# Overlapping the first attention block with the LayerNorm and V prologue, with V computed by head group

## The chip, the cores and the metric

The kernel runs on one core of one Trainium2 chip. The metric is the device time of one execution in microseconds (us), as a median of several executions. All executions used here agree within about 0.7% per kernel. ScalarE is written ACT in the profile, VectorE is DVE, GpSimd is POOL, TensorE is PE with its weight loads apart as PEld, and the DMA queue is SP.

## The reference

The sum of three terms is computed for x of 1x2048x512 in bfloat16:

```python
xn = layernorm(x)
q, k, v = split(xn @ wqkv)            # 32 heads of 16
A = concat_heads(softmax(q k^T / 4) v) @ wo
h = layernorm(xn)                      # "LN2" below
u = gelu(einsum("bsd,sf->bdf", h, w1) + b1)
B = (einsum("bdf,fs->bds", u, w2) + b2).transpose(0, 2, 1)
out = x + A + B
```

## The kernel before

A host-side scheduler writes one instruction list per engine, and every engine executes its list in order. A dependence between engines becomes a semaphore wait in front of the later instruction. So an instruction waits for all that was *emitted* before it on its own engine, whether it needs it or not.

The attention has 32 blocks of four heads. A block has 16 *periods*. In each period TensorE computes four score tiles (two pairs), ScalarE takes two exps of 128x1024, and TensorE multiplies the exps of two periods earlier with V ("PV"). Up to two further matmuls of 512 columns per period are taken from a queue of extra tasks: the K projection of later head groups (`kt`), Q projections (`qt`), the feed-forward parts (`ut`, `yt`) and the output projection (`op`). These share one PSUM bank (`EX_BANK`), so the next task's matmul waits until VectorE has evicted the one before.

The parts that matter (cut):

```python
def ln_stats(t, which):     # VectorE: statistics; POOL: (var + eps) ** -0.5
    dve.bn_stats(...); dve.bn_aggr(...)
    pool.tensor_scalar(... EPS ...); pool.tensor_tensor(... ALU.pow)
def ln_norm(t, which):      # VectorE, waits for POOL
    dve.tensor_scalar(dst[:, t, :], src[:, t, :], mean, rstd, ALU.subtract, ALU.mult)

# prologue, all 16 tiles before the first exp
for s_ in range(NT + 4):
    if s_ < NT: ln_stats(s_, 0)                        # statistics of the new tile first
    t = s_ - 1: ln_norm(t, 0); transpose_pe(t, t % 2)  # then the previous tile's normalize
    t = s_ - 2: transpose_copy(...); v_pe(t, ...); kt_pe(0, t // 4, ...) every fourth
    t = s_ - 3: v_evac(t, ...); kt_evac(...) every fourth
qt_proj(0, 0, EX_BANK)
late_consts()               # POOL: two memsets of wo_pad, then its loads

def task_ln2():             # one tile per period, from period 0 of block 0
    for t in range(NT):
        yield 0.0
        ln_stats(t, 1); ln_norm(t, 1)

# main loop, per period: scores, two exps, PV of period-2, then extra tasks
def exp_pair(n):
    act.activation(pT[:, buf, :], ps[...1024 columns...], ACTF.Exp, scale=0.25)
```

The softmax here doesn't subtract the row's maximum and nothing guards it: scores larger than these inputs give would overflow.

Of the kernel before, what the change touches and what calls it, by code (L numbers as in the profile page):

```python
# [13 lines left out]
D = 512  # L14
# [166 lines left out]
def bass_parallel_sum__softmax_full_mha__mixer_token_mlp__prompt_kernel(  # L181
# [18 lines left out]
    with ExitStack() as es:  # L200
# [48 lines left out]
        def bank(i):  # L249
            return ps[:, i * 512:(i + 1) * 512]  # L250
# [21 lines left out]
        sc.add("pool", lambda e: e.memset(mhalf[:], -0.5), writes=[("mhalf",)])  # L272
        sc.add("dve", lambda e: e.memset(b1c_bf[:], 0.0), writes=[("b1c",)])
        v17_main = V17[:, 0:NKT * H * 17].rearrange("p (n c) -> p n c", c=17)
        sc.add("dve", lambda e: e.memset(v17_main[:, :, 16:17], 1.0), writes=[("Vone",)])
        sc.add("dve", lambda e: e.memset(V17[:, NKT * H * 17:], 0.0), writes=[("Vpad",)])

        sc.add("pool", lambda e: e.memset(qmask[:, 0:1], 0.0), writes=[("qmask",)])
        for r in range(4):
# [72 lines left out]
        def transpose_pe(t, bk):  # L352
            for ct in range(NCT):
                sc.add("pe", lambda e, ct=ct: e.transpose(  # L354
                    ps_bf[:, bk * 1024 + ct * 128: bk * 1024 + (ct + 1) * 128],
                    xn_sb[:, t, ct * 128:(ct + 1) * 128], ident[:]),
                    reads=[("xn", t), ("ident",)], writes=[("bank", bk)])

        def transpose_copy(t, bk, eng):
            dst = xnT[:, :, t * 128:(t + 1) * 128]  # L360
            src = ps_bf[:, bk * 1024: bk * 1024 + 512].rearrange("p (ct j) -> p ct j", ct=NCT)
            evac(eng, dst, src, reads=[("bank", bk)], writes=[("xnT", t)])
# [10 lines left out]
        def kt_pe(T, c, bk):  # L373
            for _ in kt_pe_gen(T, c, bk):
                pass
# [10 lines left out]
        def evac(eng, dst, src, reads, writes):  # L386
            if eng == "act":
                return sc.add("act", lambda e: e.activation(dst, src, ACTF.Identity), reads=reads, writes=writes)  # L388
            return sc.add("dve", lambda e: e.tensor_copy(dst, src), reads=reads, writes=writes)  # L389
# [18 lines left out]
                                                                        None, ALU.mult),  # L408
                       reads=[("bank", bk), ("qmask",)], writes=[("QT", slot)])

        def v_tile(t, bk, evac_eng="dve"):
            v_pe(t, bk)
            v_evac(t, bk, evac_eng)

        def v_evac(t, bk, evac_eng):
            dst = V17[:, t * H * 17:(t + 1) * H * 17].rearrange("p (h c) -> p h c", c=17)[:, :, 0:16]
            src = bank(bk).rearrange("p (h d) -> p h d", d=16)
            evac(evac_eng, dst, src, reads=[("bank", bk)], writes=[("V", t)])

        def v_pe(t, bk):  # L420
            for ct in range(NCT):
                sc.add("pe", lambda e, ct=ct: e.matmul(  # L422
                    bank(bk), lhsT=xnT[:, ct, 128 * t:128 * (t + 1)], rhs=wqkv_sb[:, ct, 2 * D:3 * D],
                    start=(ct == 0), stop=(ct == NCT - 1)),
                    reads=[("wqkv", 2), ("xnT", t)], writes=[("bank", bk)])

        for s_ in range(NT + 4):
            if s_ < NT:
                ln_stats(s_, 0)
            t = s_ - 1  # L430
            if 0 <= t < NT:
                ln_norm(t, 0)
                transpose_pe(t, t % 2)
            t = s_ - 2
            if 0 <= t < NT:
                transpose_copy(t, t % 2, "act")
                v_pe(t, 2 + (t % 2))
                if t % 4 == 3:
                    kt_pe(0, t // 4, 4 + ((t // 4) % 2))
            t = s_ - 3  # L440
            if 0 <= t < NT:
                v_evac(t, 2 + (t % 2), "dve" if t % 4 == 1 else "act")
                if t % 4 == 3:
                    kt_evac(0, t // 4, 4 + ((t // 4) % 2), "act")
        qt_proj(0, 0, EX_BANK)
        late_consts()

        def task_ln2():
            for t in range(NT):
# [3 lines left out]
        def task_qt(arg):  # L453
            qb, T = arg
            yield from qt_proj_gen(qb, T, EX_BANK)

        def task_kt(T):
            for c in range(4):
# [154 lines left out]
            T, e_ = divmod(G, 2)  # L613
            return b, kt, qb, G, T, e_

        def score_group(g):
            b, kt, qb, G, T, e_ = blk_of(g)
            slot_q = b % NQS
            for r in range(4):
                n = 2 * g + r // 2  # L620
                s_ = n % 3
                bk = 2 * s_ + (r % 2)
                sc.add("pe", lambda e, r=r, bk=bk: e.matmul(  # L623
                    bank(bk), lhsT=KT[32 * r:32 * r + 32, T, 128 * kt:128 * (kt + 1)],
                    rhs=QT[32 * r:32 * r + 32, slot_q, :], start=True, stop=True,
                    tile_position=(32 * r, 0)),
                    reads=[("KT", T, kt // 4), ("QT", slot_q)], writes=[("bank", bk)], name="sc")

        def exp_pair(n):
            s_ = n % 3  # L630
            buf = n % NPB
            sc.add("act", lambda e: e.activation(pT[:, buf, :], ps[:, s_ * 1024:(s_ + 1) * 1024], ACTF.Exp, scale=0.25),  # L632
                   reads=[("bank", 2 * s_), ("bank", 2 * s_ + 1)], writes=[("pT", buf)], name="exp")

        def pv_group(g):
            b, kt, qb, G, T, e_ = blk_of(g)
            for r in range(4):
                n = 2 * g + r // 2
                buf = n % NPB
                h = 8 * T + 2 * r + e_  # L640
                off = (kt * H + h) * 17
                sc.add("pe", lambda e, r=r, buf=buf, off=off: e.matmul(  # L642
                    bank(PV_BANK)[32 * r:32 * r + 32, :], lhsT=V17[:, off:off + 32],
                    rhs=pT[:, buf, 512 * (r % 2):512 * (r % 2 + 1)],
                    start=(kt == 0), stop=(kt == NKT - 1), tile_position=(0, 32 * r)),
                    reads=[("V", kt), ("pT", buf), ("Vone",)] + ([("V", kt + 1)] if kt + 1 < NKT else [("Vpad",)]),
                    writes=[("bank", PV_BANK)], name="pv")

        def P(b, kt=0):
            return b * NKT + kt  # L650
# [5 lines left out]
                if b > 0:  # L656
                    sched_list.append((P(b - 1, 1), 0, "qt", (qb, T)))
        for T in range(1, 4):
            sched_list.append((P(2 * T - 2, 2), 1, "kt", T))
        for ft in range(NFT):  # L660
            sched_list.append((P(1, 4) + 6 * ft, 2, "ut", ft))
        for st in range(NT):
# [9 lines left out]
        def start_task(kind, arg):  # L672
            if kind == "qt":
                return task_qt(arg)
            if kind == "kt":
                return task_kt(arg)
            if kind == "ut":
                return task_ut(arg)
            if kind == "yt":
                return task_yt(arg)  # L680
            if kind == "op":
                return task_outproj(*arg)
            raise ValueError(kind)
# [9 lines left out]
                self.req = next(self.gen, None)  # L693

        bank_q = []
        free_tasks = [Task("ln2", None, task_ln2())]
        sl_idx = 0
        w1_loaded = 0
        w2_loaded = 0
        period = 0  # L700
        END = NGRP + LAG + 1
        while True:
            if period == P(0, 8):
                for ft in range(min(NW1, NFT)):
                    task_w1_load(ft)
                w1_loaded = min(NW1, NFT)
            if period == P(3, 0):
                for st in range(min(NW2, NT)):
                    task_w2_load(st)
                w2_loaded = min(NW2, NT)  # L710
            if period < NGRP:
                score_group(period)
                exp_pair(2 * period)
                exp_pair(2 * period + 1)
            for gp in (period - LAG - 1, period - LAG):
                if not (0 <= gp < NGRP):
                    continue
                b, kt = divmod(gp, NKT)
                due = gp + LAG + (1 if (kt == 0 and b > 0) else 0)
                if due != period:  # L720
                    continue
                pv_group(gp)
                if kt == NKT - 1:
                    if b == NBLK - 1:
                        assert sl_idx >= len(sched_list) and not any(tk.kind == "op" for tk in bank_q), \
                            "pre-accumulation of the last q block must be complete before the tail"
                        tail_epilogue(b)
                    else:
                        epilogue_copy(b)
                        free_tasks.append(Task("epi", b, task_epilogue_rest(b)))  # L730
            while sl_idx < len(sched_list) and sched_list[sl_idx][0] <= period:
                _, _, kind, arg = sched_list[sl_idx]
                tk_new = Task(kind, arg, start_task(kind, arg))
                if kind in ("qt", "kt"):
                    pos_ins = 1 if bank_q and bank_q[0].started else 0
                    while pos_ins < len(bank_q) and bank_q[pos_ins].kind in ("qt", "kt"):
                        pos_ins += 1
                    bank_q.insert(pos_ins, tk_new)
                else:
                    bank_q.append(tk_new)  # L740
                sl_idx += 1
# [93 lines left out]
```

## Time and profile before

| | before |
|---|---|
| median of 6 runs | 1007.68 us (1007.08 to 1010.33) |
| span of the profiled run | 1005.3 us |
| ScalarE busy | 968.6 us (96%) |
| first exp starts | 38.07 us |
| exp 32 (block 1) starts, counted from the timeline | 70.5 us |
| exp 72 starts, counted likewise | 108.9 us |

Exps are numbered from 0 to 1023. These lines of the profile page give busy time of the engines, the chain of work that ended last (by line), and the group of the exps.

```profile
PE 859.5 (85%) x4832; PEld 194.9 (19%) x4832; DVE 293.4 (29%) x472; ACT 968.6 (96%) x1068; POOL 71.0 (7%) x110
...
ACT pT L632 81%; PE ps L623 3%; PE ps L642 2%; PE ps L399 1%; DVE stats L329 1%; DVE big L344 1%; PE ps L484 1%; PE ps L422 1%; POOL mv L335 1%; PE ps L530 1%; ACT ga_sb L499 1%; PE ps L381 0%; DVE mv L331 0%; POOL mv L333 0%; DMA x_sb<-in_
...
L632 ACT ACTIVATE pT<-ps 128x1024 bf16<-128x1024 f32 x1024 | 946.6, 1307 | 8.7 <-PE ps L623 6.6
```

81% of the chain is the exp. Undisturbed, exps pass one every 0.918 us (107 in 98.24 us in the chain of waits), so a period costs 1.84 us and all 1024 cost 940 us. The rest of the time lies before the first exp, in gaps between exps, and in the tail. The next lines are ScalarE's timeline (start, duration, instruction, count of merged instructions, and in brackets the idle time before and what ended it).

```profile
38.07 13.29 ACT L632 ACTIVATE pT<-ps 128x1024 bf16<-128x1024 f32 x14 [1.50 <-PE ps L623]
51.77 3.77 ACT L632 ACTIVATE pT<-ps 128x1024 bf16<-128x1024 f32 x4 [0.41 <-PE ps L623]
57.47 20.56 ACT L632 ACTIVATE pT<-ps 128x1024 bf16<-128x1024 f32 x22 [1.93 <-PE ps L623]
78.75 17.08 ACT L632 ACTIVATE pT<-ps 128x1024 bf16<-128x1024 f32 x18 [0.72 <-PE ps L623]
95.57 0.77 ACT L499 ACTIVATE ga_sb<-ga_sb 128x512 f32<-128x512 f32 x1
96.09 14.41 ACT L632 ACTIVATE pT<-ps 128x1024 bf16<-128x1024 f32 x15
```

The first exp starts at 38.07 us. Gaps of 0.41, 1.93 and 0.72 us follow in block 0. Block 0's cause stands in VectorE's timeline, with one LN2 tile and the copy that ends the block:

```profile
29.20 3.61 DVE L344 TENSOR_SCALAR big<-x_sb,mv 128x512 bf16<-128x512 bf16 x1 [0.77 <-POOL mv L335]
...
42.77 0.69 DVE L329 BATCH_NORM_STATS2 stats<-big 128x6 f32<-128x512 bf16 x1
43.49 0.18 DVE L331 BATCH_NORM_AGGREGATE mv<-stats 128x2 f32<-128x6 f32 x1
44.67 0.41 DVE L344 TENSOR_SCALAR big<-big,mv 128x512 bf16<-128x512 bf16 x1 [1.00 <-POOL mv L335]
...
76.39 0.68 DVE L566 COPY OT<-ps 128x512 f32<-128x512 f32 x1
```

One LN2 tile is statistics (42.77), aggregation (43.49), 1.00 us of idling for POOL, normalize (44.67); the next tile starts 2.23 us after the first. 16 tiles and four evictions of KT fill VectorE from 38.31 to 76.39 us, where block 0's PV bank is copied. In front of each of the last three KT evictions stand two LN2 tiles, so they are 5.06 us apart where four exps take 3.67 us; that is block 0's loss, and run i below removes it. The line at 29.20 is different: a normalize that takes 0.41 us elsewhere took 3.61 us. POOL's timeline shows what ran at that moment:

```profile
29.12 3.55 POOL L315 MEMSET wo_pad<- 128x2048 bf16 x2
```

These are the two `wo_pad` memsets. The Trainium skill ("SBUF — State Buffer", "SBUF: two separate sides") says that VectorE and GpSimd share a port pair by an exclusive lock that is held for the whole instruction. The trace agrees: 3.61 us beside 3.55.

### The profile page before, as it was taken

The page shows a single profiled execution, that of the slowest core. Times are in us where ns is not written, and L with a number is a line of the kernel's source. Part 1 is how long each engine was busy: PE and PEld are TensorE (multiplying, and loading weights), DVE is VectorE, ACT ScalarE, POOL GpSimd, SP SyncE. Part 2 cuts the span into 40 slices and gives each one's busy share as a digit, 9 for nine tenths or more (in the row PEclk, how much of TensorE's full clock was granted, in tenths as well). Part 3 has the DMA queues.
Part 4 walks back from the last instruction along what each step waited for, and adds up shares of the span by engine and source line. Part 5 has one row for each costly group of instructions (what it writes and reads, how often), then busy time and mean ns, then how long its engine had stood idle before and what let it go on. Part 6 is the DMA issues. An engine that isn't in the chain of part 4 may idle for free.

```text
span 1005.3 us, 11492 instructions
## 1 busy us (share of the span) xinstructions
PE 859.5 (85%) x4832; PEld 194.9 (19%) x4832; DVE 293.4 (29%) x472; ACT 968.6 (96%) x1068; POOL 71.0 (7%) x110
## 2 busy tenths in 40 slices
PE   6788888887888888888888888999989888999986
PEld 3211121211112122222222211111111211111111
DVE  6653333223323313332222322121122322112223
ACT  5799999999999999999999999999999999999995
POOL 5430000000000000000000000000000000000000
PEclk9867898978789799999899975555555955555586
DMA  5110200011100011100110000000000000000000
GB/s 147 37 27 22 50 22 22 1 22 42 22 17 1 15 29 29 31 23 26 29 29 15 11 11 1 0 1 1 1 1 1 17 6 1 0 1 1 1 1 22
DMA packets 55428, 18.31 MB, mean 18 GB/s; under 512 B 49232, under 2 KB 55376, under 8 KB 55376
## 3 DMA queue, kind: packets, MB, share of 16 engines
q1 hardware_dynamic: 55376, 17.58, 7.4%
q8 instruction: 38, 0.62, 0.3%
q14 instruction: 14, 0.11, 0.0%
HBM read 15.47 MB, written 2.10 MB: 17 GB/s over the span
## 4 chain that ended last, share of the span: by engine, by line
ACT 82%; PE 11%; DVE 4%; POOL 1%; issue 1%; DMA 0%; SPq 0%; ACTq 0%
ACT pT L632 81%; PE ps L623 3%; PE ps L642 2%; PE ps L399 1%; DVE stats L329 1%; DVE big L344 1%; PE ps L484 1%; PE ps L422 1%; POOL mv L335 1%; PE ps L530 1%; ACT ga_sb L499 1%; PE ps L381 0%; DVE mv L331 0%; POOL mv L333 0%; DMA x_sb<-in_A_x_dram 0%
## 5 line engine op out<-in xcount | busy, mean ns | idle before, releaser
L632 ACT ACTIVATE pT<-ps 128x1024 bf16<-128x1024 f32 x1024 | 946.6, 1307 | 8.7 <-PE ps L623 6.6
L623 PE MATMUL ps<-QT,KT 32*128 32x512 bf16 x2048 | 457.6, 483 | 119.6 <-ACT pT L632 96.7
L642 PE MATMUL ps<-pT,V 128*32 128x512 bf16 x2048 | 250.8, 491 | 1.7 <-DVE OT L566 1.2
L623 PEld LDWEIGHTS ps<-QT,KT 32*128 32x128 bf16 x2048 | 94.5, 94 | 525.4 <-ACT pT L632 505.8
L566 DVE COPY OT<-ps 128x512 f32<-128x512 f32 x31 | 21.4, 692 | 350.8 <-PE ps L642 350.8
L578 DVE RECIPROCAL denb<-denb 128x128 f32<-128x128 f32 x124 | 107.8, 919 | 0.9
L581 POOL TENSOR_TENSOR oT<-OT,denb 128x512 bf16<-128x512 f32 x31 | 39.3, 1267 | 861.8 <-DVE denb L578 861.8
L642 PEld LDWEIGHTS ps<-pT,V 128*32 128x32 bf16 x2048 | 52.3, 98 | 158.9 <-issue 155.3
L484 PE MATMUL ps<-big,w1blk 128*128 128x512 bf16 (+1 forms) x176 | 61.4, 435 | 1.4 <-DVE QT L407 1.4
L511 PE MATMUL ps<-gT,w2blk 128*128 128x512 bf16 (+1 forms) x176 | 57.7, 404 | 1.3 <-DVE QT L407 1.3
L516 DVE SCALAR_TENSOR_TENSOR big<-ps,x_sb 128x512 f32<-128x512 f32 x16 | 11.1, 691 | 106.8 <-PE ps L511 106.8
L530 PE MATMUL ps<-wo_pad,oT 128*128 128x512 bf16 x120 | 40.2, 420 | 0.4 <-DVE QT L407 0.4
L407 DVE TENSOR_SCALAR QT<-ps,qmask 128x512 bf16<-128x512 f32 x32 | 22.6, 748 | 31.9 <-PE ps L399 31.9
L399 PE MATMUL ps<-xnT,wqkv_sb 128*128 128x512 bf16 x64 | 28.2, 539 | 0.0
L543 DVE TENSOR_TENSOR osb<-ps,big 128x512 bf16<-128x512 f32 x16 | 11.0, 689 | 57.7 <-PE ps L530 57.6
L381 PE MATMUL ps<-xnT,wqkv_sb 128*128 128x512 bf16 x64 | 22.7, 453 | 3.4 <-DVE KT L389 3.4
L489 DVE TENSOR_SCALAR u_sb<-ps,b1col 128x512 f32<-128x512 f32 (+1 forms) x11 | 8.2, 749 | 58.1 <-PE ps L484 58.1
L573 DVE STREAM_SHUFFLE denb<-OT 128x512 f32<-128x512 f32 x31 | 22.5, 724 | 0.0
L388 ACT ACTIVATE xnT<-ps 128x512 bf16<-128x512 bf16 x16 | 9.5, 595 | 11.8 <-PE ps L354 11.8
L335 POOL TENSOR_TENSOR mv<-mv,mhalf 128x1 f32<-128x1 f32 x32 | 18.2, 570 | 2.7
L422 PE MATMUL ps<-wqkv_sb,xnT 128*128 128x512 bf16 x64 | 18.0, 409 | 0.0
L354 PE MATMUL ps<-ident,big 128*128 128x128 bf16 x64 | 6.9, 237 | 11.7 <-DVE big L344 11.7
(49 smaller groups left out, 184.0 us busy)
## 6 DMA issues: line engine op xcount, KB each, us to landing
w1blk<-in_B_w_dram SPq DMA_DIRECT2D x10, 512.0 KB, 4.1
w2blk<-in_B_w_dram SPq DMA_DIRECT2D x16, 320.0 KB, 3.4
out_dram<-osb SPq DMA_DIRECT2D x16, 128.0 KB, 1.7
wqkv_sb<-in_A_wqkv_dram SPq DMA_DIRECT2D x3, 512.0 KB, 6.0
x_sb<-in_A_x_dram SPq DMA_DIRECT2D x3, 512.0 KB, 7.0
wo_pad<-in_A_wo_dram SPq DMA_DIRECT2D x8, 64.0 KB, 2.0
w2blk<-in_B_w_dram SPq DMA_DIRECT2D x16, 24.0 KB, 1.7
w1blk<-in_B_w_dram SPq DMA_DIRECT2D x1, 384.0 KB, 3.9
```

What stands on the lines that cost most here:

```text
L335: sc.add("pool", lambda e: e.tensor_tensor(mv[:, i, 2:3], mv[:, i, 1:2], mhalf[:], ALU.pow), reads=[("mv", i), ("mhalf",)], writes=[("mv", ...
L381: sc.add("pe", lambda e, ct=ct: e.matmul(bank(bk), lhsT=wqkv_sb[:, ct, D + 128 * T: D + 128 * T + 128], rhs=xnT[:, ct, 512 * c:512 * (c + ...
L399: sc.add("pe", lambda e, ct=ct: e.matmul(bank(bk), lhsT=wqkv_sb[:, ct, 128 * T:128 * (T + 1)], rhs=xnT[:, ct, 512 * qb:512 * (qb + 1)], st ...
L422: sc.add("pe", lambda e, ct=ct: e.matmul(bank(bk), lhsT=xnT[:, ct, 128 * t:128 * (t + 1)], rhs=wqkv_sb[:, ct, 2 * D:3 * D], start=(ct == 0 ...
L484: sc.add("pe", lambda e, st=st: e.matmul(bank(EX_BANK)[0:m, :], lhsT=w1blk[:, slot, st, 0:m], rhs=h_sb[:, st, :], start=(st == 0), stop=(s ...
L511: sc.add("pe", lambda e, ft=ft, m=m: e.matmul(bank(EX_BANK), lhsT=w2blk[0:m, slot, ft, :], rhs=gT[0:m, ft, :], start=(ft == 0), stop=(ft = ...
L530: sc.add("pe", lambda e, G=G: e.matmul(bank(EX_BANK), lhsT=oT[:, par, G, 128 * sti:128 * (sti + 1)], rhs=wo_pad[:, G, :], start=(G == 0), ...
L578: sc.add("dve", lambda e, cs=cs: e.reciprocal(denb[:, eb, cs], denb[:, eb, cs]), reads=[("denb", eb, c)], writes=[("denb", eb, c)])
L581: sc.add("pool", lambda e: e.tensor_tensor(oT[:, qb % 2, G, :], OT32[:, eb, :], denb[:, eb, :], ALU.mult), reads=[("OT32", eb)] + [("denb" ...
L623: sc.add("pe", lambda e, r=r, bk=bk: e.matmul(bank(bk), lhsT=KT[32 * r:32 * r + 32, T, 128 * kt:128 * (kt + 1)], rhs=QT[32 * r:32 * r + 32 ...
L632: sc.add("act", lambda e: e.activation(pT[:, buf, :], ps[:, s_ * 1024:(s_ + 1) * 1024], ACTF.Exp, scale=0.25), reads=[("bank", 2 * s_), (" ...
L642: sc.add("pe", lambda e, r=r, buf=buf, off=off: e.matmul(bank(PV_BANK)[32 * r:32 * r + 32, :], lhsT=V17[:, off:off + 32], rhs=pT[:, buf, 5 ...
```

## The change

The intent is to shorten the prologue. Only 10 prologue stages run before the first exp; the other 9 run one per period inside block 0. Only the V columns of head group 0 are computed there, and groups 1 to 3 follow as queued tasks (`vt`) in blocks 1, 2 and 4. LN2 moves from block 0 to block 1, and so does the K projection of head group 1 (`kt`, four chunks with one eviction each). To free two PSUM banks, the ring of score pairs has two slots instead of three in block 0. The core of the diff (cut):

```diff
-        sc.add("dve", lambda e: e.memset(v17_main[:, :, 16:17], 1.0), writes=[("Vone",)])
-        sc.add("dve", lambda e: e.memset(V17[:, NKT * H * 17:], 0.0), writes=[("Vpad",)])
+        sc.add("dve", lambda e: e.memset(V17[:, :], 0.0), ...)
+        sc.add("dve", lambda e: e.memset(v17_main[:, :, 16:17], 1.0), ...)
...
-        for s_ in range(NT + 4):
-            if s_ < NT:
-                ln_stats(s_, 0)
...
+        def pro_stage(s_, pre):
+            ev = "act" if pre else "dve"
+            t = s_ - 3
+            if 0 <= t < NT:
+                vT_evac([t], 0, vb(t), ev if t % 2 == 0 else "dve")
+                if t % 4 == 3:
+                    kt_evac(0, t // 4, kb(t), ev)
+            t = s_ - 2
+            if 0 <= t < NT:
+                transpose_copy(t, tb(t), ev)
+                vT_pe([t], 0, vb(t))
+                if t % 4 == 3:
+                    kt_pe(0, t // 4, kb(t))
+                    if t == 3:
+                        qt_proj(0, 0, EX_BANK)
             t = s_ - 1
             if 0 <= t < NT:
                 ln_norm(t, 0)
-                transpose_pe(t, t % 2)
+                transpose_pe(t, tb(t))
+            t = s_
+            if 0 <= t < NT:
+                ln_stats(t, 0)
+        NSTG_PRE = NPRE + 3 + SH            # 4 + 3 + 3
+        for s_ in range(NSTG_PRE):
+            pro_stage(s_, True)
         late_consts()
+        def block0_work(period):
+            pro_stage(period + NSTG_PRE, False)
...
-            sched_list.append((P(2 * T - 2, 2), 1, "kt", T))
+            sched_list.append((P(max(2 * T - 2, 1), 0), 1, "kt", T))
+            for j in range(4):
+                sched_list.append((P(max(2 * T - 2, 1), 1) + 3 * j, 1, "vt", (T, j)))
...
-        free_tasks = [Task("ln2", None, task_ln2())]
+        free_tasks = []
...
+            if period == P(1, 0):
+                free_tasks.append(Task("ln2", None, task_ln2()))
...
+            if period < NKT:
+                block0_work(period)
```

More of the change, by code (lines that the diff above doesn't have):

```diff
@@ L274, in bass_parallel_sum__softmax_full_mha__mixer_token_mlp__prompt_kernel @@
         v17_main = V17[:, 0:NKT * H * 17].rearrange("p (n c) -> p n c", c=17)
-        sc.add("dve", lambda e: e.memset(v17_main[:, :, 16:17], 1.0), writes=[("Vone",)])
-        sc.add("dve", lambda e: e.memset(V17[:, NKT * H * 17:], 0.0), writes=[("Vpad",)])
+        sc.add("dve", lambda e: e.memset(V17[:, :], 0.0), writes=[("Vpad",)] + [("Vone",)] +
+               [("V", t, T) for t in range(NT) for T in range(4)])
+        sc.add("dve", lambda e: e.memset(v17_main[:, :, 16:17], 1.0), reads=[("Vone",)], writes=[("Vone",)])
         sc.add("pool", lambda e: e.memset(qmask[:, 0:1], 0.0), writes=[("qmask",)])
@@ L409, in qt_proj_gen @@
                        reads=[("bank", bk), ("qmask",)], writes=[("QT", slot)])
-        def v_tile(t, bk, evac_eng="dve"):
-            v_pe(t, bk)
-            v_evac(t, bk, evac_eng)
-        def v_evac(t, bk, evac_eng):
-            dst = V17[:, t * H * 17:(t + 1) * H * 17].rearrange("p (h c) -> p h c", c=17)[:, :, 0:16]
-            src = bank(bk).rearrange("p (h d) -> p h d", d=16)
-            evac(evac_eng, dst, src, reads=[("bank", bk)], writes=[("V", t)])
-        def v_pe(t, bk):
-            for ct in range(NCT):
-                sc.add("pe", lambda e, ct=ct: e.matmul(
-                    bank(bk), lhsT=xnT[:, ct, 128 * t:128 * (t + 1)], rhs=wqkv_sb[:, ct, 2 * D:3 * D],
-                    start=(ct == 0), stop=(ct == NCT - 1)),
-                    reads=[("wqkv", 2), ("xnT", t)], writes=[("bank", bk)])
@@ L427, in bass_parallel_sum__softmax_full_mha__mixer_token_mlp__prompt_kernel, with vT_pe @@
-        for s_ in range(NT + 4):
-            if s_ < NT:
-                ln_stats(s_, 0)
+        def vT_pe(tiles, T, bk):
+            for j, t in enumerate(tiles):
+                for ct in range(NCT):
+                    sc.add("pe", lambda e, ct=ct, j=j, t=t: e.matmul(
+                        bank(bk)[:, 128 * j:128 * (j + 1)], lhsT=xnT[:, ct, 128 * t:128 * (t + 1)],
+                        rhs=wqkv_sb[:, ct, 2 * D + 128 * T:2 * D + 128 * (T + 1)],
+                        start=(ct == 0), stop=(ct == NCT - 1)),
+                        reads=[("wqkv", 2), ("xnT", t)], writes=[("bank", bk)])
@@ new lines, in vT_evac @@
+        def vT_evac(tiles, T, bk, evac_eng):
+            n = len(tiles)
+            t0_ = tiles[0]
+            assert tiles == list(range(t0_, t0_ + n))
+            dst = V17[:, t0_ * H * 17:(t0_ + n) * H * 17].rearrange("p (t h c) -> p t h c", t=n, c=17)[:, :, 8 * T:8 * T + 8, 0:16]
+            src = bank(bk)[:, 0:128 * n].rearrange("p (t h d) -> p t h d", t=n, d=16)
+            evac(evac_eng, dst, src, reads=[("bank", bk)], writes=[("V", t, T) for t in tiles])
+        NPRE = 4
+        SH = 3
@@ new lines, in tb, with vb, kb @@
+        def tb(t):
+            return t % 2 if t < NPRE else 4
+        def vb(t):
+            return 2 + (t % 2) if t < NPRE else 5
+        def kb(t):
+            return PV_BANK if t < NPRE else EX_BANK
+        def pro_stage(s_, pre):
[13 more added lines that the diff above has]
+                        qt_proj(0, 0, EX_BANK)
@@ L432, in bass_parallel_sum__softmax_full_mha__mixer_token_mlp__prompt_kernel @@
                 ln_norm(t, 0)
-                transpose_pe(t, t % 2)
-            t = s_ - 2
+                transpose_pe(t, tb(t))
+            t = s_
             if 0 <= t < NT:
-                transpose_copy(t, t % 2, "act")
-                v_pe(t, 2 + (t % 2))
-                if t % 4 == 3:
-                    kt_pe(0, t // 4, 4 + ((t // 4) % 2))
-            t = s_ - 3
-            if 0 <= t < NT:
-                v_evac(t, 2 + (t % 2), "dve" if t % 4 == 1 else "act")
-                if t % 4 == 3:
-                    kt_evac(0, t // 4, 4 + ((t // 4) % 2), "act")
-        qt_proj(0, 0, EX_BANK)
+                ln_stats(t, 0)
+        NSTG_PRE = NPRE + 3 + SH
+        for s_ in range(NSTG_PRE):
+            pro_stage(s_, True)
         late_consts()
+        def block0_work(period):
+            pro_stage(period + NSTG_PRE, False)
         def task_ln2():
@@ L455, in task_qt, with task_vt @@
             yield from qt_proj_gen(qb, T, EX_BANK)
+        def task_vt(arg):
+            T, j = arg
+            tiles = list(range(4 * j, 4 * j + 4))
+            for i, t in enumerate(tiles):
+                yield 1.0
+                vT_pe_one = (lambda tt, ii: [sc.add("pe", lambda e, ct=ct: e.matmul(
+                    bank(EX_BANK)[:, 128 * ii:128 * (ii + 1)], lhsT=xnT[:, ct, 128 * tt:128 * (tt + 1)],
+                    rhs=wqkv_sb[:, ct, 2 * D + 128 * T:2 * D + 128 * (T + 1)],
+                    start=(ct == 0), stop=(ct == NCT - 1)),
+                    reads=[("wqkv", 2), ("xnT", tt)], writes=[("bank", EX_BANK)]) for ct in range(NCT)])
+                vT_pe_one(t, i)
+            yield 0.0
+            vT_evac(tiles, T, EX_BANK, "dve")
         def task_kt(T):
@@ L614, in blk_of, with pslot, score_group @@
             return b, kt, qb, G, T, e_
-        def score_group(g):
+        def pslot(n):
+            return n % 2 if n < 2 * NKT else n % 3
+        def score_group(g, rs=(0, 1, 2, 3)):
             b, kt, qb, G, T, e_ = blk_of(g)
             slot_q = b % NQS
-            for r in range(4):
+            for r in rs:
                 n = 2 * g + r // 2
-                s_ = n % 3
+                s_ = pslot(n)
                 bk = 2 * s_ + (r % 2)
@@ L629, in exp_pair @@
         def exp_pair(n):
-            s_ = n % 3
+            s_ = pslot(n)
             buf = n % NPB
@@ L645, in pv_group @@
                     start=(kt == 0), stop=(kt == NKT - 1), tile_position=(0, 32 * r)),
-                    reads=[("V", kt), ("pT", buf), ("Vone",)] + ([("V", kt + 1)] if kt + 1 < NKT else [("Vpad",)]),
+                    reads=[("V", kt, T), ("pT", buf), ("Vone",)] + (
+                        [("V", kt, T + 1)] if T < 3 else ([("V", kt + 1, 0)] if kt + 1 < NKT else [("Vpad",)])),
                     writes=[("bank", PV_BANK)], name="pv")
@@ L676, in start_task @@
                 return task_kt(arg)
+            if kind == "vt":
+                return task_vt(arg)
             if kind == "ut":
@@ L710, in bass_parallel_sum__softmax_full_mha__mixer_token_mlp__prompt_kernel @@
                 w2_loaded = min(NW2, NT)
-            if period < NGRP:
+            if period < NKT:
+                score_group(period, (0, 1))
+                exp_pair(2 * period)
+                score_group(period, (2, 3))
+                exp_pair(2 * period + 1)
+            elif period < NGRP:
                 score_group(period)
@@ L730, in bass_parallel_sum__softmax_full_mha__mixer_token_mlp__prompt_kernel @@
                         free_tasks.append(Task("epi", b, task_epilogue_rest(b)))
+            if period < NKT:
+                block0_work(period)
             while sl_idx < len(sched_list) and sched_list[sl_idx][0] <= period:
@@ L733, in bass_parallel_sum__softmax_full_mha__mixer_token_mlp__prompt_kernel @@
                 tk_new = Task(kind, arg, start_task(kind, arg))
-                if kind in ("qt", "kt"):
+                if kind in ("qt", "kt", "vt"):
                     pos_ins = 1 if bank_q and bank_q[0].started else 0
-                    while pos_ins < len(bank_q) and bank_q[pos_ins].kind in ("qt", "kt"):
+                    while pos_ins < len(bank_q) and bank_q[pos_ins].kind in ("qt", "kt", "vt"):
                         pos_ins += 1
```

## The prediction

> **What bounds it now.** The chain of waits is 81% ScalarE exp (L632): 1024 exps of 128x1024, which undisturbed pass at 0.918 us each (107 in 98.24 us), so a period of two takes 1.84 us, 940 us in all. The window table shows ScalarE about 99% busy from 100 to 950 us. What is left to gain is the prologue: the timeline has the first exp at 38.07 us. Block 0 then loses some 4 us, because the second LayerNorm (LN2) paces VectorE: 38.31 to 76.39 us for 16 tiles and four KT evictions. One LN2 tile takes 2.23 us, 1.00 us of it VectorE idle for POOL.
>
> **What the change does.**
> 1. Prologue: 9 tiles instead of 16 before the first exp, but three things cost time:
>  - The V memset grows from 512 elements (0.485 us) to 4360 32-bit words. The Trainium skill ("VectorE: DVE Perf Modes", zero memsets) says one cycle per element; scaled from this trace, an estimate of 4.1 us. First statistics move from 2.86 to about 7.3 us.
>  - Statistics were emitted before the previous tile's normalize, hiding POOL's 1.0 us; now they follow it. Unobstructed tiles took 1.18 us, now I expect 2.23.
>  - At tile 3 VectorE waits for the Q projection, about +3 us.
>  So normalize(8) ends near 30.4 and the first exp starts near **31.3 us**: only 7 us saved.
> 2. Block 0. The wo_pad memsets on POOL (3.55 us) held a normalize for 3.61 us (at 29.20). The skill ("SBUF — State Buffer", "SBUF: two separate sides": the shared port pair is an exclusive lock) explains this; now they meet normalize(9) and leave ScalarE idle about 4 us after the first two exps. Then six stages run at VectorE's pace (2.23 us, +1.5 us where a KT chunk is evicted), the rest at 1.85. Block 1 starts near 68.5 us (before: exp 32 at 70.5).
> 3. Block 1 is where the gain is lost. LN2 moved here: 16 x 2.23 + 8 evictions of KT and V (0.62) + epilogue of block 0 (copy, shuffle, four reciprocals, 4.8) + QT (1.4) = about 47 us of in-order VectorE work, against 29.4 us of exps. PE waits for that queue through the extra bank and the copy of the PV bank. The copy of block 1's PV bank lands near 117 us, and exp 72 follows at 118 us, against 109 before (one tanh already paid there). Net about **+10 us**.
> 4. V matmuls of head groups 1 to 3: 192 more weight loads, 8 narrow matmuls of about 0.1 us for two of 0.215 us; 0 to 3 us in all. Feed-forward work shifts two blocks later; I expect it still hidden.
>
> **Predicted: 1018 us**, 1008 to 1030 in 8 of 10. Faster by over 2%: 0.02; within 2%: 0.87; slower by over 2%: 0.11.
>
> **What would show it.** First exp at 29 to 33 us; normalize idle 1.00 us on POOL in the prologue; one normalize of about 3.6 us in block 0; exps in block 1 about 1.3 us apart, PE's waits there put down to VectorE copies (KT, V, OT); from about 130 us on ScalarE over 99% busy as before.
>
> **What would make it wrong.** A faster V memset (up to 4 us better); LN2 tiles starting early in block 0's idle end; a lower granted clock while feed-forward matmuls run: at 0.6 a period with two extra matmuls took 2.06 us, so 20 us more would be possible.

## The result

| | before | after |
|---|---|---|
| median | 1007.75 us (16 runs) | 1020.74 us (7 runs, 1018.31 to 1022.48) |
| span of the profiled run | 1005.3 us | 1019.3 us |
| first statistics | 2.86 us | 7.35 us |
| first exp | 38.07 us | 34.81 us |
| exp 32 | 70.5 us | 70.5 us |
| exp 72 | 108.9 us | 121.8 us |
| from exp 72 to the end of the span | 896.4 us | 897.5 us |

The ratio is 1.0122 with a 95% interval of 1.0109 to 1.0134. A ratio is the mean time of one kernel's fast runs over that of the other kernel's fast runs of the same rounds, so it is not quite the ratio of the medians quoted. An eighth run of the changed kernel, 1022.53 us, is not in its median. The difference is under 2%, but the interval is clear of 1. The change made the kernel about 13 us slower, and all of it is lost before exp 72. (Exp 32 and exp 72 lie inside merged lines of the timeline and are counted from these: 57.47 + 14 x 0.931 and 55.61 + 16 x 0.934 for exp 32, 96.09 + 14 x 0.918 and 116.30 + 6 x 0.918 for exp 72. Before had already paid for one `tanh` by exp 72, some 0.5 us from 95.57 to 96.09, which the changed kernel pays later; that is half of the last row's difference.)

The page of the changed kernel, the same lines as before:

```profile
PE 848.8 (83%) x5024; PEld 206.2 (20%) x5024; DVE 309.8 (30%) x503; ACT 958.0 (94%) x1049; POOL 69.4 (7%) x110
...
ACT pT L673 80%; PE ps L664 3%; PE ps L683 2%; PE ps L522 1%; DVE big L345 1%; DVE stats L330 1%; POOL mv L336 1%; PE ps L400 1%; PE ps L382 1%; DVE QT L408 1%; PE ps L568 1%; ACT ga_sb L537 1%; POOL mv L334 1%; PE ps L549 0%; DVE mv L332 0
...
L673 ACT ACTIVATE pT<-ps 128x1024 bf16<-128x1024 f32 x1024 | 948.0, 1378 | 26.5 <-PE ps L664 24.1
```

The exps are as long in sum as before (948.0 beside 946.6 us), but the idle time before them rose from 8.7 to 26.5 us. ScalarE's timeline shows where:

```profile
34.81 1.94 ACT L673 ACTIVATE pT<-ps 128x1024 bf16<-128x1024 f32 x2 [3.38 <-PE ps L664]
38.61 1.94 ACT L673 ACTIVATE pT<-ps 128x1024 bf16<-128x1024 f32 x2 [1.86 <-PE ps L664]
...
47.67 7.59 ACT L673 ACTIVATE pT<-ps 128x1024 bf16<-128x1024 f32 x8 [2.24 <-PE ps L664]
55.61 24.36 ACT L673 ACTIVATE pT<-ps 128x1024 bf16<-128x1024 f32 x26 [0.34 <-PE ps L664]
82.51 4.00 ACT L673 ACTIVATE pT<-ps 128x1024 bf16<-128x1024 f32 x4 [2.55 <-PE ps L664]
...
95.97 4.00 ACT L673 ACTIVATE pT<-ps 128x1024 bf16<-128x1024 f32 x4 [2.79 <-PE ps L664]
...
111.77 4.00 ACT L673 ACTIVATE pT<-ps 128x1024 bf16<-128x1024 f32 x4 [1.82 <-PE ps L664]
116.30 14.77 ACT L673 ACTIVATE pT<-ps 128x1024 bf16<-128x1024 f32 x16 [0.53 <-PE ps L664]
```

The first exp comes 3.3 us earlier. The gaps of block 0 then use this up: exp 32, inside the line at 55.61, starts at 70.5 us in both kernels. Block 1 loses the rest. From 82.51 to 111.77 us, ScalarE runs four exps and then waits, over and over.

VectorE's timeline in the prologue and at the start of block 0:

```profile
1.73 3.69 DVE L275 MEMSET V<- 128x4360 uint32 x1 [0.87 <-issue]
...
7.35 0.64 DVE L330 BATCH_NORM_STATS2 stats<-x_sb 128x6 f32<-128x512 bf16 x1
...
15.89 0.41 DVE L345 TENSOR_SCALAR big<-x_sb,mv 128x512 bf16<-128x512 bf16 x1 [0.82 <-POOL mv L336]
...
21.72 1.41 DVE L408 TENSOR_SCALAR QT<-ps,qmask 128x512 bf16<-128x512 f32 x2 [4.60 <-PE ps L400]
23.04 0.40 DVE L345 TENSOR_SCALAR big<-x_sb,mv 128x512 bf16<-128x512 bf16 x1
...
34.78 3.01 DVE L345 TENSOR_SCALAR big<-x_sb,mv 128x512 bf16<-128x512 bf16 x1
```

The V memset at 1.73 us puts off the first statistics to 7.35 us. Nearly every normalize waits 0.82 to 1.00 us for POOL (15.89), because the statistics of the next tile are now emitted after it. At 21.72 VectorE has stood still for 4.60 us in front of the two masked Q evictions, so the normalize of tile 4 follows that of tile 3 by 7.15 us instead of 2.23. At 34.78 the normalize of tile 9 takes 3.01 us beside the `wo_pad` memsets. What VectorE waited for at 21.72 is TensorE:

```profile
18.06 1.91 PE L382 MATMUL ps<-xnT,wqkv_sb 128*128 128x512 bf16 x4
19.76 1.91 PE L400 MATMUL ps<-xnT,wqkv_sb 128*128 128x512 bf16 x4
```

Four matmuls of 512 columns start 1.70 us before the next four, so each takes 0.43 us. In the kernel before, four of the same matmuls took 0.86 us, as its chain of waits shows:

```profile
14.91 0.86 PE ps L381 x4
```

The Trainium skill ("TensorE: Matmul & The Clock Gate", "Wait — 56ns, not 53.3ns?") gives 426.7 ns for 512 columns while the array is cold and 215.7 ns once it is warm. The trace agrees with both figures. So TensorE is still cold at 18 us, where in the kernel before it was warm at 14.9. Why is not shown, and a lighter prologue alone does not explain it: in run h below, with the same share of the projections in front, TensorE is busy about as long from 10 to 20 us (6.26 us beside 6.25 here), and there the four Q matmuls at 17.32 took 0.86 us.

VectorE in block 1, the KT evictions and the copy of the block's PV bank:

```profile
73.68 0.68 DVE L390 CAST KT<-ps 128x512 bf16<-128x512 f32 x1
...
80.21 0.63 DVE L390 CAST KT<-ps 128x512 bf16<-128x512 f32 x1
...
93.63 0.68 DVE L390 CAST KT<-ps 128x512 bf16<-128x512 f32 x1
...
117.40 0.68 DVE L604 COPY OT<-ps 128x512 f32<-128x512 f32 x1
```

Between two KT evictions there are 6.5 to 6.8 us. In front of each stand two LN2 tiles, as in block 0 of the kernel before, and now pieces of the epilogue of block 0 as well: a shuffle and a reciprocal, then two reciprocals, then one (there the second normalize, at 92.36, took 1.34 us, beside a multiply of 1.26 us on POOL). TensorE cannot begin the next chunk in the shared bank before, and it does not reach the next scores either, since it too executes in order. The waits between 65 and 125 us (who waited for whom, total, count, longest) agree: LN2's normalize waits 15 times 1.0 us for POOL, TensorE waits up to 3.2 us at a time for KT, and ScalarE waits 12.6 us for scores.

```profile
DVE big L345 <- POOL mv L336: 15.0, 15, 1.0
...
ACT pT L673 <- PE ps L664: 12.6, 7, 2.8
...
PEld ps L382 <- DVE KT L390: 7.1, 4, 3.2
```

One rival can be settled from this trace. TensorE's granted clock was only 0.50 from 82 to 100 us. But from the copy of block 0's PV bank at 73.07 to that of block 1's at 117.40, VectorE's timeline shows no wait for TensorE, only for POOL. A faster TensorE would not have brought an eviction forward.

### The profile page after: what moved, and what is told of

It reads as the page before. It is cut to its first block, busy times and chain, and to the rows that moved or that the text cites. A ratio compares the mean times of both kernels' runs of the same rounds, so it can differ in the third digit from the quotient of the medians.

```text
span 1019.3 us, 11887 instructions
## 1 busy us (share of the span) xinstructions
PE 848.8 (83%) x5024; PEld 206.2 (20%) x5024; DVE 309.8 (30%) x503; ACT 958.0 (94%) x1049; POOL 69.4 (7%) x110
## 4 chain that ended last, share of the span: by engine, by line
ACT 81%; PE 10%; DVE 6%; POOL 2%; issue 1%; ACTq 0%
ACT pT L673 80%; PE ps L664 3%; PE ps L683 2%; PE ps L522 1%; DVE big L345 1%; DVE stats L330 1%; POOL mv L336 1%; PE ps L400 1%; PE ps L382 1%; DVE QT L408 1%; PE ps L568 1%; ACT ga_sb L537 1%; POOL mv L334 1%; PE ps L549 0%; DVE mv L332 0%
## 5 line engine op out<-in xcount | busy, mean ns | idle before, releaser
L673 ACT ACTIVATE pT<-ps 128x1024 bf16<-128x1024 f32 x1024 | 948.0, 1378 | 26.5 <-PE ps L664 24.1
L664 PE MATMUL ps<-QT,KT 32*128 32x512 bf16 x2048 | 442.7, 471 | 121.6 <-ACT pT L673 103.7
L683 PE MATMUL ps<-pT,V 128*32 128x512 bf16 x2048 | 244.0, 478 | 0.6 <-ACT pT L673 0.6
L554 DVE SCALAR_TENSOR_TENSOR big<-ps,x_sb 128x512 f32<-128x512 f32 x16 | 11.1, 691 | 108.9 <-PE ps L549 108.9
L486 PE MATMUL ps<-wqkv_sb,xnT 128*128 128x128 bf16 x192 | 16.4, 234 | 6.2 <-DVE V L390 4.6
L389 ACT ACTIVATE xnT<-ps 128x512 bf16<-128x512 bf16 x8 | 4.8, 597 | 17.8 <-PE ps L355 17.8
```

The source lines that it names most:

```text
L664: sc.add("pe", lambda e, r=r, bk=bk: e.matmul(bank(bk), lhsT=KT[32 * r:32 * r + 32, T, 128 * kt:128 * (kt + 1)], rhs=QT[32 * r:32 * r + 32 ...
L673: sc.add("act", lambda e: e.activation(pT[:, buf, :], ps[:, s_ * 1024:(s_ + 1) * 1024], ACTF.Exp, scale=0.25), reads=[("bank", 2 * s_), (" ...
L683: sc.add("pe", lambda e, r=r, buf=buf, off=off: e.matmul(bank(PV_BANK)[32 * r:32 * r + 32, :], lhsT=V17[:, off:off + 32], rhs=pT[:, buf, 5 ...
```

## The experiments

The first theory is that of the prediction: VectorE's in-order work in block 1 paces TensorE and with it ScalarE. Rival 1 is that the V split costs it: 192 more weight loads, narrow matmuls, twelve evictions. Rival 2 is the two-slot score ring of block 0, or the later feed-forward work. All results were correct. Each batch had its own runs of the kernel before.

| run | median us | ratio to before, 95% interval |
|---|---|---|
| after (the change) | 1020.74 | 1.0122 [1.0109, 1.0134] |
| a_ln2_pipe | 1007.40 | 0.9988 [0.9965, 1.0010] |
| b_ln2_early | 1015.68 | 1.0072 [1.0057, 1.0088] |
| c_pro_order | 1015.76 | 1.0067 [1.0036, 1.0098] |
| d_vt_alone (on before) | 1008.34 | 1.0004 [0.9982, 1.0026] |
| e_wo_late | 1017.17 | 1.0089 [1.0071, 1.0106] |
| f_qt_later | 1018.15 | 1.0093 [1.0074, 1.0111] |
| g_memset | 1016.45 | 1.0082 [1.0066, 1.0098] |
| h_all | 993.31 | 0.9855 [0.9836, 0.9875] |
| i_before_fixed (on before) | 1003.83 | 0.9940 [0.9922, 0.9958] |
| j_ln2_slow | 1009.39 | 0.9997 [0.9974, 1.0020] |
| k_all_sh1 | 990.36 | 0.9818 [0.9798, 0.9837] |

### a: LN2 with statistics one tile ahead

```diff
+            yield 0.0
+            ln_stats(0, 1)
             for t in range(NT):
                 yield 0.0
-                ln_tile(t, 1)
+                if t + 1 < NT:
+                    ln_stats(t + 1, 1)
+                ln_norm(t, 1)
```

> Changed kernel, with one edit: LN2 takes the statistics of tile t+1 before the normalize of tile t, so VectorE no longer sits idle 1.00 us per tile for POOL. Theory (block 1 is paced by VectorE's in-order queue, 47 us of work against 29.4 us of exps): 15 us of idle leave that queue, the copy of block 1's PV bank comes about 12 us earlier (near 105 us instead of 117), and the time falls to 1005 to 1010 us. Rival 1 (the many narrow V matmuls and their evictions cost it): no change, 1018 to 1021. Rival 2 (the score ring of two slots in block 0, or the late feed-forward work): no change either.

Measured: 1007.40 us, 13 us less than the change. The same work in another order on one engine removed the whole loss. ScalarE's timeline in block 1:

```profile
84.26 3.77 ACT L677 ACTIVATE pT<-ps 128x1024 bf16<-128x1024 f32 x4 [0.61 <-PE ps L668]
88.55 4.00 ACT L677 ACTIVATE pT<-ps 128x1024 bf16<-128x1024 f32 x4 [0.51 <-PE ps L668]
93.15 58.02 ACT L677 ACTIVATE pT<-ps 128x1024 bf16<-128x1024 f32 x63 [0.60 <-PE ps L668]
```

The gaps of 2.55 to 2.79 us have become 0.5 to 0.6 us. The copy of block 1's PV bank starts at 104.33 us instead of 117.40, in VectorE's timeline:

```profile
104.33 0.69 DVE L608 COPY OT<-ps 128x512 f32<-128x512 f32 x1
```

Both rivals expected no change and are out as the main cause.

### b: LN2 starts early

```diff
-            if period == P(1, 0):
+            if period == P(0, 9):
                 free_tasks.append(Task("ln2", None, task_ln2()))
```

> Changed kernel, with one edit: LN2 starts at period 9 of block 0 instead of period 0 of block 1, so that VectorE's idle 15 us at the end of block 0 (58 to 73 us) take 6 or 7 of the 16 tiles. Theory of VectorE's queue: block 1 loses 14 us of VectorE work, time 1005 to 1010 us. Rival 1 and rival 2: no change, 1018 to 1021.

Measured: 1015.68 us. The direction was right, but the size was not: 5 us instead of the 10 to 15 expected. ScalarE's timeline shows why:

```profile
82.19 3.77 ACT L673 ACTIVATE pT<-ps 128x1024 bf16<-128x1024 f32 x4 [2.52 <-PE ps L664]
89.50 4.00 ACT L673 ACTIVATE pT<-ps 128x1024 bf16<-128x1024 f32 x4 [3.54 <-PE ps L664]
...
102.06 49.14 ACT L673 ACTIVATE pT<-ps 128x1024 bf16<-128x1024 f32 x53 [1.77 <-PE ps L664]
```

VectorE did take half of LN2 in its idle time before block 1, but the gaps in the first half of block 1 are as large as before. Only those in the second half are gone. What counts is therefore not the sum of VectorE's work in the block. It is the work queued in front of each eviction that TensorE waits for. In the first half there are still two LN2 tiles and one or two pieces of the epilogue in front of each KT chunk, however many tiles were done earlier, and the KT evictions are still 6.5 to 6.7 us apart. This corrects the theory.

### j: LN2 early, and one tile in every second period

```diff
+            if period == P(0, 9):       # as in b
             for t in range(NT):
                 yield 0.0
+                yield 0.0
                 ln_tile(t, 1)
```

> Changed kernel, with LN2 from period 9 of block 0 on, as in the run before that started it early, but one tile every second period (periods 9 to 41), its POOL wait of 1.00 us kept. Theory as corrected by that run (what counts is not the sum of VectorE's work in block 1 but how much of it is queued between two evictions that TensorE waits for: 2 LN2 tiles and a reciprocal between two KT chunks are 6.7 us, against three periods of 1.84 us): with half the LN2 tiles per period the queue keeps up, ScalarE gaps in block 1 under 1 us each, 1006 to 1010 us. Theory as first stated (the sum counts): as when started early, 1014 to 1017 us.

Measured: 1009.39 us, inside the range of the corrected theory and outside that of the first one. The POOL wait of 1.00 us was kept. Between the copies of the PV banks of block 0 and block 1, VectorE's timeline has eight LN2 tiles here and eight in b, so the sum in block 1 is the same and only the rate differs. The copies are 31.6 us apart here (72.77 and 104.33) and 40.1 in b (73.41 and 113.53). VectorE's KT evictions:

```profile
73.72 0.69 DVE L390 CAST KT<-ps 128x512 bf16<-128x512 f32 x1 [0.26 <-PE ps L382]
...
78.03 0.63 DVE L390 CAST KT<-ps 128x512 bf16<-128x512 f32 x1
...
86.99 0.68 DVE L390 CAST KT<-ps 128x512 bf16<-128x512 f32 x1
```

They are 4.3 to 4.5 us apart instead of 6.5 to 6.8. Two gaps of ScalarE remain there (0.71 and 1.18 us; under 1 us was expected). The expectation speaks of three periods per chunk; the timelines show four exps, so two periods, between gaps. So 4.3 us is still a little over the 3.67 us that four exps take.

### d: the V tasks alone, on the kernel before

```diff
+            for j in range(4):
+                sched_list.append((P(max(2 * T - 2, 1), 1) + 3 * j, 1, "vt", (T, j)))
```

(with `task_vt`, its eviction and the finer dependence keys of the change; V is computed twice and the same values are written again)

> Kernel before, with the V work of the changed kernel added on top and nothing else: head groups 1 to 3 of V are computed a second time by the narrow matmuls (192 more, with their weight loads and twelve evictions of 128x512) at the same periods of blocks 1, 2 and 4 as in the changed kernel; prologue, LN2 and score ring as before. The result stays right, since the same values are written again. Theory: 0 to 3 us slower than before (1008 to 1011). Rival 1 (the split of V is what costs): 8 us or more slower.

Measured: 1008.34 us against 1008.20 in the same rounds, ratio 1.0004. The narrow matmuls and their evictions cost nothing that can be seen where VectorE is not already behind. Rival 1 is out.

### c, e, f, g: the four losses of the prologue, one at a time

c emits statistics first in each stage:

```diff
             ev = "act" if pre else "dve"
+            t = s_
+            if 0 <= t < NT:
+                ln_stats(t, 0)
             t = s_ - 3
...
-            t = s_
-            if 0 <= t < NT:
-                ln_stats(t, 0)
```

> Changed kernel, with one edit: each prologue stage takes the statistics of the new tile first and the normalize of the one before it after that, as the kernel before did. Theory: the prologue's 1.00 us of POOL latency per tile is hidden again in 8 or 9 stages, first exp near 27 us instead of 34.8, the six VectorE-paced stages of block 0 fall from 2.23 to under 1.9 us; block 1 is moved earlier as a whole and still loses 18 us; time 1009 to 1013 us. If instead the prologue were bound by TensorE or by the input loads, the first exp stays after 32 us and the time above 1017.

Measured: first exp at 31.90 us and 1015.76 us (1011.22 to 1017.81, the widest range here). The time lies between the two that were expected. The first exp moved by 2.9 us, where 8 were expected. The Q wait stayed (5.43 us), and a second limit came up. TensorE's list alternates transposes with V matmuls, which wait for ScalarE's copy of the transposes. TensorE's transposes of the first tiles, with VectorE no longer late:

```profile
9.66 0.61 PE L355 MATMUL ps<-ident,big 128*128 128x128 bf16 x4 [9.66 <-DVE big L345]
...
11.43 0.63 PE L355 MATMUL ps<-ident,big 128*128 128x128 bf16 x4
...
13.15 0.63 PE L355 MATMUL ps<-ident,big 128*128 128x128 bf16 x4
```

They are 1.7 us apart on a cold array, with a wait for the copy in each, so the prologue could not get down to VectorE's 1.18 us per tile.

e moves the `wo_pad` memsets and loads to the start of block 3:

```diff
-        late_consts()  # with wo_pad memsets and loads
+            if period == P(3, 0):
+                wo_consts()
```

> Changed kernel, with one edit: the two wo_pad memsets on POOL (3.55 us) and their loads move from the end of the prologue to the start of block 3, where nothing on VectorE uses the shared port pair often. Theory (the memsets hold normalize(9) for 3.0 us through the port lock, and that leaves ScalarE idle): normalize(9) takes 0.41 us, the 1.86 us of ScalarE idle after the first two exps goes, all later work moves 2 to 2.7 us earlier, 1018 to 1019 us. If the lock is not the cause, normalize(9) still takes about 3 us and the time stays.

Measured: 1017.17 us. The normalize of tile 9 in VectorE's timeline:

```profile
34.78 0.40 DVE L347 TENSOR_SCALAR big<-x_sb,mv 128x512 bf16<-128x512 bf16 x1
```

It starts at the same time as in the changed kernel and takes 0.40 us instead of 3.01. The first six exps run without a gap. So it is the memsets that hold it, and not the loads that moved with them: in the changed kernel the first of these is issued at 37.67 us, after the memsets end at 37.65. That the port lock is the means was not tested apart; it is the account of the Trainium skill quoted above, and the durations fit it. The time fell by 3.6 us between medians, a little more than expected.

f moves the Q projection from tile 3's stage to tile 5's and its evictions to the stage after:

```diff
-                    if t == 3:
-                        qt_proj(0, 0, EX_BANK)
+                if t == 5:
+                    qt_pe0()      # matmuls; qt_evac0() one stage later
```

> Changed kernel, with one edit: the Q projection of block 0 moves from the stage of tile 3 to that of tile 5, and its two masked evictions to the stage after, so that VectorE does not stand 4.60 us before them. Theory (this wait is a 5 us hole in the prologue's chain): first exp at 30 to 31 us instead of 34.8, block 1 starts as much earlier and loses as much as before, 1016 to 1018 us. If TensorE, not VectorE, sets the prologue's pace there (its matmuls of 512 columns take 0.43 us at this point), the first exp gains under 2 us.

Measured: first exp at 28.66 us, 6.2 us earlier than in the changed kernel and earlier than expected, and 1018.15 us, just outside the 1016 to 1018 expected. About 2 us of this came back at once, since the `wo_pad` memsets then held the normalize of tile 9 for 3.43 us with less to hide it (a ScalarE gap of 3.91 us instead of 1.86). The profiled run (1015.77 us) is the fastest of the four; the others took 1018.05 to 1019.26 us, and where they lost the rest is not shown.

g sets only the columns to zero that are read before they are written:

```diff
-        e.memset(V17[:, :], 0.0)
+        vnext = V17[:, 0:NKT * H * 17].rearrange("p (t g c) -> p t g c", t=NKT, g=4)[:, :, 1:4, 0:16]
+        e.memset(vnext, 0.0); e.memset(V17[:, NKT * H * 17:], 0.0)
```

> Changed kernel, with one edit: instead of all of V17 (4360 words, statistics held until 7.35 us) only the first 16 columns of head groups 1 to 3 of each tile are set to zero, the only ones read before they are written. Theory (the memset is serial with the whole prologue): first statistics near 3.9 us, first exp near 31.3 us, 1016.5 to 1018 us. If the input loads or TensorE set the pace, the first exp gains under 1.5 us.

Measured: first statistics at 3.11 us, first exp at 30.56 us, 1016.45 us. The memset was serial with everything after it: 4.24 us at the first statistics are 4.25 us at the first exp.

### h: all of these together

> Changed kernel, with all edits together: LN2 with statistics one tile ahead and starting at period 9 of block 0; prologue stages with statistics first; wo_pad memsets late; Q projection later; V memset cut. Theory (the overlap is worth having once VectorE's queue is short): first exp at 21 to 25 us, no ScalarE gap of over 1 us after block 0 has started, 990 to 998 us, faster than both kernels. Rival (the overlap itself costs as much as it gains, through the score ring of two slots and TensorE work inside block 0): 1003 us or more.

Measured: 993.31 us, faster than both kernels. ScalarE's timeline up to 130 us:

```profile
23.10 7.44 ACT L693 ACTIVATE pT<-ps 128x1024 bf16<-128x1024 f32 x8 [1.90 <-PE ps L684]
31.26 7.44 ACT L693 ACTIVATE pT<-ps 128x1024 bf16<-128x1024 f32 x8 [0.72 <-PE ps L684]
39.19 28.02 ACT L693 ACTIVATE pT<-ps 128x1024 bf16<-128x1024 f32 x30 [0.49 <-PE ps L684]
68.18 62.66 ACT L693 ACTIVATE pT<-ps 128x1024 bf16<-128x1024 f32 x68 [0.98 <-PE ps L684]
```

The first exp starts at 23.10 us, and no later gap reaches 1 us. This run also uses the two-slot ring for exps 0 to 31. The 30 exps from 39.19 us, of which 16 are in block 0, take 28.02 us, or 0.934 each; the 22 from 57.47 us in the kernel before, with three slots, took 20.56 us, or 0.935. So the ring costs nothing visible there, which answers that part of rival 2. The ratios of a, c, e, f and g fall by 0.0134, 0.0055, 0.0033, 0.0029 and 0.0040 from that of the change. Their sum, 0.0291, would give 0.983 for all. 0.9855 was measured, so the single effects nearly add up. (b is left out of the sum; it shortens the same queue as a.)

### i: the kernel before with two of the repairs

```diff
 (edit a, and edit e, on the kernel before: no overlap, V undivided)
```

> Kernel before (no overlap, V undivided), with two of the edits alone: LN2 takes statistics one tile ahead, and the wo_pad memsets move to the start of block 3. It asks what the overlap itself is worth, against the run with all edits (993.3 us). Theory: the 3.6 us hold of the last prologue normalize goes (first exp near 34.5 us instead of 38.07), and block 0 loses almost none of its 4 us, since VectorE's LN2 work falls from 38 to about 23 us: 999 to 1002 us, so that of the 15 us won by all edits the overlap with its own repairs keeps 6 to 9. If the repairs are all there is to win and the overlap nothing: 995 us or less.

Measured: 1003.83 us. The 58 exps from 36.17 us on run without a gap, so LN2 with statistics ahead costs block 0 nothing. The first exp came 1.9 us earlier, not 3.6; the last V, K and Q projections on TensorE follow the normalize, and VectorE waits 3.06 us for them. The time is neither in the range expected nor near that of the alternative. What the overlap with its own repairs is worth follows from h and i, which ran in different batches: 8.6 us by the ratios to before (0.9940 and 0.9855), 10.5 us by the medians. So it is worth about 9 to 10 us, and whether that is inside the 6 to 9 expected is not decided.

### k: all together, with two prologue stages fewer in front

```diff
-        SH = 3
+        SH = 1
```

(and the Q projection in the stage of tile 4)

> Kernel with all edits, and two prologue stages fewer before the first exp (8 instead of 10), so two tiles more inside block 0; the Q projection one tile earlier. If block 0 can take a stage in a period of 1.84 us, as the run with all edits shows it nearly does: first exp near 20 us, 990 to 992 us. If TensorE, VectorE and the KT evictions in block 0 are already at their limit, the earlier start is given back as gaps: 993 to 996 us.

Measured: 990.36 us, first exp at 21.44 us. The time is as expected, the first exp 1.4 us later. This is the fastest version here, 17 to 19 us better than the kernel before (ratio 0.9818, interval 0.9798 to 0.9837, so just on either side of 2%).

## Why the prediction was right

**The total** was 1018 us, and 1020.74 was measured, inside 1008 to 1030 and in the class of highest chance. The mechanism held: the prologue gains little, block 0 takes that away, and block 1 loses the rest to VectorE's queue, with nothing caught up later.

**Step 1, prologue.** First statistics near 7.3 us: 7.35, partly by luck, since the memset took 3.69 us instead of 4.1, and two idle times in front of it and of the memset of ones (0.87 and 1.80 us, against 1.69 in the kernel before) made up for it. POOL wait of 1.00 us back in nearly each stage: 0.82 to 1.00. That term was right. The Q projection was sized at +3 us and measured +4.9 (7.15 instead of 2.23 us between two normalizes), and the K projection of tiles 4 to 7 put some 1.5 us more between normalize(8) and the first exp. Most of both errors has one source: these matmuls ran at 0.43 us instead of 0.215, their warm duration in the profile of before. For the twelve in the chain that is 2.6 us of the 3.5 by which the first exp was missed (an estimate from these durations; the text does not say how it costed them). So normalize(8) ended at 32.4 instead of 30.4, and the first exp came at 34.81 instead of 31.3, outside the 29 to 33 given.

**Step 2, block 0.** One normalize of about 3.6 us: 3.01, and e showed the memsets behind it. The gap on ScalarE was 1.86 us instead of 4: the first exps came 3.5 us later than predicted, the memsets only about 2 (an estimate; they follow the statistics of tile 9, and normalize(8) before these was 2 us late), and the hold was 0.6 us shorter. The stages after it ran at VectorE's pace as predicted: normalizes 2.23 us apart, and 3.57 where a KT chunk was evicted. Block 1 began at 70.5 us instead of 68.5.

**Step 3, block 1.** The copy of its PV bank came at 117.40 us (117 predicted), exp 72 at 121.8 (118), 30 exps from 82.51 to there at 1.31 us each (1.3). a and j show the cause. That the copy came on time is in part luck: the block began 2 us late, and VectorE's work from one copy to the next took 44.3 us instead of 47. But the reason given, a sum of 47 us of work against 29.4 us of exps, was only half right. b took much of that sum away and won only 5 us. It is the queue in front of each eviction that TensorE needs. In the changed kernel both readings give the same number, because the queue never runs empty there. "LN2 tiles starting early" was listed as something that would make the prediction wrong; it did not happen, and b shows that it would have helped less than thought.

**Step 4, the V split and the later feed-forward work.** 0 to 3 us predicted; d measured nothing. From exp 72 to the end both kernels need the same time within 1.1 us. No run moved the feed-forward work alone, so that part rests on this comparison.

## What to carry to other kernels

Where engines execute in order, ask of each piece of work that you move what will stand behind it in its new queue; slack on average does not help an eviction that has 6.5 us of unrelated work in front of it and 3.7 us of time. A wait on another engine inside a pair of instructions is removed by emitting the next item's first half in between; here that one reordering was worth 13 us, and losing it in the prologue cost 5. When a prologue is changed, do not carry the warm matmul times of the old one over (here 0.43 us instead of 0.215), and look at the overlap again once its small losses are gone: the same overlap lost 13 us as first written and won 14 to 19 us together with its repairs, of which two of the repairs alone give some 6 us (i).

## What the Trainium skill lacked or had wrong

- "TensorE: Matmul & The Clock Gate": its cold and warm times for 512 columns agree with the trace (0.43 and 0.215 us). The page calls the ramp penalty less than 1% of a typical kernel's span and advises against fitting a count of cold matmuls. It is less here too, but it made up some 2.6 us of the 3.5 us error at the first exp, nearly as much as the change gained there (3.3 us). The profile's table of windows showed a granted clock of 1.00 from 10 to 20 us, in which matmuls of 512 columns took 0.43 us. So the granted clock does not tell cold from warm here. The page warns that clock events in traces can be unreliable, but does not have this case.
- "VectorE: DVE Perf Modes", zero memsets: the memset was issued in the 32-bit form that the page describes. The record of the 4360-word memset shows 3.69 us, 0.85 ns per word, less than the 4.1 us scaled from the small one of before.
- No page has the idle time of about 1.7 us on VectorE, put down to "issue", in front of the memset of ones (1.69 us in the kernel before, 1.80 in the changed one, 1.68 in h). Its cause is open.
- "SBUF — State Buffer": the exclusive lock is borne out (3.01, 3.43 and 3.61 us for a normalize of 0.41). The page does not say that two memsets back to back on GpSimd keep a waiting VectorE instruction out for both: 3.61 us beside 3.55 for the two.
